# Layer 2's weights decoded in place, part of their lower halves on VectorE, and the first loads on ScalarE's queue, in a top-k attention and two-layer gated network kernel

## The chip, the cores and the metric

The program runs on one core of a Trainium2 chip. The metric is the device time of one execution in microseconds (us); the time before is 1244.49 us, the median of three runs (1243.4 to 1245.45). TensorE (PE in the profile) multiplies matrices into PSUM, VectorE (DVE), ScalarE (ACT) and GpSimd (POOL) work element by element on 128 partitions, SyncE (SP) issues the transfers.

## The reference, cut to what matters

```python
# q, k, v: (4, 8, 576, 64); all inputs arrive as float64
scores = q @ k.T / 8
mask   = scores >= (32nd largest of each row)
attn   = softmax(where(mask, scores, -1e9))
x      = (attn @ v) as 2304 tokens x 512
# layer 1, weights 512x1536, 512x1536, 1536x512
xn = x / sqrt(mean(x*x) + 1e-6) * rms_g
x  = (silu(xn @ w_gate) * (xn @ w_val)) @ w_out
# layer 2, weights of the same sizes
out = (sigmoid(x @ w_gate2) * (x @ w_val2)) @ w_out2
```

## The kernel before, in words

Every line of the profile reads L355, since one helper records all operations (`record`) and one place issues them (`issue`). The tiles' names tell the operations apart.

**A planner sets the order.** The program is first recorded as a list of operations with a priority each. `order` then plays a list schedule: five engines, a cost per operation (`cost`), rings of buffers, and for each engine the ready operation that can start soonest and, among those, the one of the lowest priority value. The engines get the operations in that order, so each engine's queue is fixed before the run. One planner rule touched by the change is the margin for TensorE: an operation of TensorE whose input ends after 250000 ns of planned time is held back by 1000 ns more (2500 ns where the input is a transfer), `SLACK`.

**Attention.** The 2304 tokens are 18 units of 128. A unit has 8 heads; one head of one unit is here called an *attend* (144 in all). An attend is: four score matmuls into `sp`; the largest eight (`MAX8` into `m`); the exponential on ScalarE (`e`); three rounds of `MATCH_REPLACE8` into the scratch tile `w` and `MAX8` of `w` on VectorE, which give the 32nd largest score; a masked product (`e<-sp,m,e`); a split in an upper half on ScalarE and a lower half on GpSimd (`ph`); a transposing transfer (`pt`) and 28 matmuls (`pv`). The scratch `w` has two buffers, and VectorE mostly runs two attends in turn.

**Layers.** Products run in float16 with operands split in an upper and a lower half, three matmuls for each product. Layer 1 (`gate1`, `out1`: tiles `pg<-xt`, `pw<-xt`, `py<-ht`) starts for a unit when its normalised rows `xt` are transposed. Layer 2 (`gate2`, `out2`: `pg<-yt`, `pw<-yt`, `po`) reads its weights from DRAM into tiles `wl` again for each batch of two units.

**Weights.** Each layer has nine pieces: three 512-wide parts (`j`) of gate, val and out (`g`, `v`, `o`), and a piece has four chunks of 128x512. A chunk arrives as 512 KB of float64 in a tile `raw` (128x512 pairs of 32-bit words), and `load_f32` turns the pairs into float32: for layer 2 (way 1) two ScalarE passes, one VectorE operation and one GpSimd addition. `prep_piece` then finds a power-of-two scale from a matmul of the piece with itself (`wps`, `wm`, `wmt`, `wx`), and makes the halves. Layer 1's halves stay in SBUF; its lower halves come from TensorE (`wlo`). For layer 2 (`prep2`, pieces `w2g`, `w2v`, `w2o`) the decoded float32 is written into a tile `wh`, which later takes the halves in its place: ScalarE scales into `wf` and rounds `wf` into the upper half, GpSimd subtracts the upper half from `wf`, and two stores per piece (512 KB each) bring it to DRAM. `raw`, `wh` and `wl` share one ring (`wbig`, tag `w4`) of seven buffers of 4 KB a partition. `gate2` keeps its gated rows in a ring of six smaller tiles (`htp`, tag `ht2`). All transfers are issued by SyncE, in its planned order; a transfer whose buffer is still in use holds up what is behind it there.

Of the kernel before, what the change touches and what calls it, by code (L numbers as in the profile page):

```python
# [9 lines left out]
F32 = mybir.dt.float32  # L10
F16 = mybir.dt.float16
BF16 = mybir.dt.bfloat16
I32 = mybir.dt.int32
# [28 lines left out]
HELD2 = False  # L42
REACH = 100.0
# [3 lines left out]
SLACK = (1000.0, 2500.0, 250000.0)  # L47
# [12 lines left out]
AHEAD = 8  # L60

# [39 lines left out]
class _Tile:  # L101
    def __init__(self, pool, args, key, lane):
        self.pool, self.args, self.key, self.lane = pool, args, key, lane
        self.real = None
        self.uses = []
        self.left = 0
        self.end = 0.0


class _Pool:  # L110
# [3 lines left out]
    def tile(self, shape, dtype, name, tag=None, bufs=None, lane=None):  # L114

        key = tag or name
        s = self.sched
        t = _Tile(self, (shape, dtype, f"{name}_{len(s.tiles)}", key, bufs), (id(self), key), lane)
        s.tiles.append(t)
        s.rings.setdefault(t.key, {"bufs": bufs or self.default, "lanes": {}})["lanes"].setdefault(lane, []).append(t)  # L120
        shadow = s.shadow.dram_tensor(f"t{len(s.tiles)}", list(shape), dtype).ap()
        return _View(t, shadow, [], [])


class _Op:
    __slots__ = "eng calls cost lat prio deps users waits tiles start end idx new later base".split()
# [10 lines left out]
class Scheduler:  # L137
# [67 lines left out]
    def cost(self, eng, method, args, kw, writes, reads):  # L205
# [16 lines left out]
        if eng == "scalar":  # L222
            return n * 0.8333 + (51 if psum else 93) + 93 * (ptrs + ("accum_out" in kw)), 200
        if eng == "gpsimd":
            if method == "tensor_tensor":
                return (516 if n == 1 else n * (1.88 if mybir.dt.size(out.dtype) == 2 else 2.1) + 149), 100
            return n * 0.833 + (224 if n == 1 else 161 + 300 * min(ptrs, 1)), 100

# [6 lines left out]
    def order(self):  # L235
        for op in self.ops:
            op.users, op.waits, op.start, op.end, op.new, op.later = [], len(op.deps), 0.0, None, [], []
# [35 lines left out]
        def choose(reach):  # L273
            best = None
            for eng in self.ENGINES:
                pick = None
                for op in ready[eng]:
# [10 lines left out]
                    key = (max(0.0, at - now[eng] - PATIENCE), op.prio, op.idx)  # L288
# [7 lines left out]
        while len(out) < len(self.ops):  # L296
# [16 lines left out]
            if op.eng == "sync":  # L313
# [4 lines left out]
                sems = sems[1:] + [done]  # L318
                if move:
                    op.end = begin + 56  # L320
# [38 lines left out]
def topk_attention_moe_kernel(  # L359
# [48 lines left out]
    wbig = pool("wbig", 7)  # L408
# [26 lines left out]
    def load_f32(dst, src, way):  # L435


        if src.dtype == F32:
            nc.sync.dma_start(dst, src)
            return  # L440
# [5 lines left out]
        E.claim(dst)  # L446
        if way == 1:
# [6 lines left out]
            return  # L454
# [4 lines left out]
        if way == 2:  # L459

            nc.scalar.activation(lo, lo.bitcast(U32), AF.Copy, scale=2.0 ** -29)
            nc.gpsimd.tensor_tensor(out=d, in0=d, in1=lo, op=ALU.add)
            return
# [4 lines left out]
    def prep_piece(w, kind, j, g, s, i, place, held, ways):  # L468
# [5 lines left out]
        for c in range(CPJ):  # L474
            r = (c if kind == "in" else j * CPJ + c) * P
            src = w[r : r + P, j * 512 : (j + 1) * 512] if kind == "in" else w[r : r + P, :]
            fs.append((held or place)(c).bitcast(F32))
            load_f32(fs[-1], src, ways[c])

        ps = ps_m.tile([P, P], F32, name="wps", tag="mm", lane="wps")  # L480
        with E.group():
            for c in range(CPJ):
                hb = fs[c].bitcast(BF16).rearrange("p (f a) -> p f a", a=2)[:, :, 1]
# [29 lines left out]
        for c in range(CPJ):  # L513
# [29 lines left out]
    def prep1(n, j):  # L543
# [9 lines left out]
        prep_piece(w, kind, j, g, s[:, j : j + 1], i[:, j : j + 1], lambda c: t[:, c], held, WAYS[0][len(pieces)])  # L553
        pieces.append([t[:, c] for c in range(CPJ)])

    def prep2(n, j):
# [3 lines left out]
        ts = [wbig.tile([P, 2, 1024], F16, name="wh", tag="w4") for _ in range(CPJ // 2)]  # L560
        held = None
        if HELD2:
            fs = [htp.tile([P, 2, CPJ, P], F16, name="fs", tag="ht2", bufs=6, lane="fs") for _ in range(CPJ)]
            held = lambda c: fs[c].rearrange("p a m r -> p (a m r)")
        prep_piece(w, kind, j, None, s[:, j : j + 1], i[:, j : j + 1], lambda c: ts[c // 2][:, c % 2], held, WAYS[1][len(pieces)])
        for a, t in enumerate(ts):
            nc.sync.dma_start(d[a], t.rearrange("p c f -> p (c f)"))
# [121 lines left out]
    def attend(parts, sc, nsc, pv, n):  # L689
# [12 lines left out]
        w = at.tile([P, S], F32, name="w", bufs=2)  # L702
# [297 lines left out]
    xs, dests, in1, in2, ht1, ht2, w2, hsq, ys, yts, state = {}, {}, {}, {}, {}, {}, {}, {}, {}, {}, {}  # L1000
# [106 lines left out]
```

## Time and profile before

| | |
|---|---|
| median of the runs | 1244.49 us |
| the profiled execution | 1248.31 us, of which the span of the profile is 1246.5 us |
| TensorE busy | 1128.9 us (91%) |
| VectorE busy | 999.0 us (80%) |
| ScalarE busy | 859.3 us (69%) |
| GpSimd busy | 844.8 us (68%) |
| first matmul that reads layer 2's weights | at 282.8 us |

The profile is one execution. Busy time is the sum of an engine's instructions; PEclk is the clock that TensorE was granted, as a share of its full 2.4 GHz. The span begins with the first instruction that is recorded; the execution's own time is 1.8 us more.

```profile
PE   4776484779899999999999999999999999999998
POOL 5997899986666667685877576566838666772530
PEclk9898576789999999999999999999999999999999
```

Each digit is one fortieth of the span (31 us) and gives the busy share in tenths. TensorE is not full in the first ten slices, while GpSimd is (and VectorE and ScalarE are too: the table of stretches further down); from the eleventh slice on TensorE is full to the end.

### The profile page before, as it was taken

The page shows a single profiled execution, that of the slowest core. Times are in us where ns is not written, and L with a number is a line of the kernel's source. Part 1 is how long each engine was busy: PE and PEld are TensorE (multiplying, and loading weights), DVE is VectorE, ACT ScalarE, POOL GpSimd, SP SyncE. Part 2 cuts the span into 40 slices and gives each one's busy share as a digit, 9 for nine tenths or more (in the row PEclk, how much of TensorE's full clock was granted, in tenths as well). Part 3 has the DMA queues.
Part 4 walks back from the last instruction along what each step waited for, and adds up shares of the span by engine and source line. Part 5 has one row for each costly group of instructions (what it writes and reads, how often), then busy time and mean ns, then how long its engine had stood idle before and what let it go on. Part 6 is the DMA issues. An engine that isn't in the chain of part 4 may idle for free.

```text
span 1246.5 us, 41715 instructions
## 1 busy us (share of the span) xinstructions
PE 1128.9 (91%) x17020; PEld 966.5 (78%) x17020; DVE 999.0 (80%) x2571; ACT 859.3 (69%) x1536; POOL 844.8 (68%) x966
## 2 busy tenths in 40 slices
PE   4776484779899999999999999999999999999998
PEld 2333273679699789978897999699879979997976
DVE  6999989798876998799989899798579899980001
ACT  6999788876676666676966576577748666763522
POOL 5997899986666667685877576566838666772530
PEclk9898576789999999999999999999999999999999
DMA  8995886889877775679877586868676865754337
GB/s 258 284 321 160 253 235 209 207 204 240 199 159 195 180 147 126 131 161 210 183 146 181 134 192 142 194 132 163 149 169 125 196 158 111 196 122 137 137 123 259
DMA packets 323776, 225.28 MB, mean 181 GB/s; under 512 B 278400, under 2 KB 286592, under 8 KB 323584
## 3 DMA queue, kind: packets, MB, share of 16 engines
q1 hardware_dynamic: 323584, 222.62, 73.1%
q8 instruction: 133, 2.18, 0.7%
q14 instruction: 59, 0.48, 0.1%
HBM read 147.06 MB, written 14.16 MB: 129 GB/s over the span
## 4 chain that ended last, share of the span: by engine, by line
PE 55%; DVE 14%; ACT 13%; issue 6%; POOL 6%; DMA 5%; SPq 2%; ACTq 0%; DVEq 0%; POOLq 0%
PE pg L355 14%; PE pw L355 14%; PE po L355 10%; PE py L355 8%; DVE m L355 5%; DVE w L355 5%; PE sp L355 3%; PE pv L355 3%; POOL ph L355 2%; SPq L355 2%; ACT raw L355 1%; ACT e L355 1%; ACT sg L355 1%; POOL sg L355 1%; DVE e L355 1%
## 5 line engine op out<-in xcount | busy, mean ns | idle before, releaser
L355 DVE MAX8 m<-w 128x8 f32<-128x576 f32 x432 | 315.0, 749 | 1.7
L355 PEld LDWEIGHTS <-wl 128*128 128x128 f16 x5184 | 292.5, 98 | 6.1 <-issue 4.7
L355 POOL TENSOR_TENSOR ph<-e,ph 128x512 f16<-128x512 f32 (+1 forms) x288 | 204.6, 735 | 77.5 <-ACT ph L355 75.9
L355 DVE MATCH_REPLACE8 w<-m,w 128x576 f32<-128x576 f32 x288 | 213.0, 742 | 0.0
L355 ACT ACTIVATE e<-sp,nb,sc 128x576 f32<-128x576 f32 x144 | 116.5, 829 | 75.5 <-POOL nb L355 41.7
L355 POOL TENSOR_TENSOR sg<-sg,sv 128x512 f32<-128x512 f32 x105 | 133.9, 1277 | 44.5 <-ACT sv L355 41.9
L355 PE MATMUL pg<-xt,w1g 128*128 128x128 f16 x2592 | 156.9, 221 | 1.2 <-DMA xt<-sn 0.4
L355 PE MATMUL pg<-yt,wl 128*128 128x128 f16 x2592 | 153.7, 219 | 3.6 <-ACT g L355 3.2
L355 PEld LDWEIGHTS <-w1v 128*128 128x128 f16 (+1 forms) x2640 | 150.1, 98 | 8.0 <-POOL w1v L355 4.3
L355 PEld LDWEIGHTS <-w1g 128*128 128x128 f16 (+1 forms) x2624 | 152.6, 99 | 3.6 <-issue 2.3
L355 PEld LDWEIGHTS <-w1o 128*128 128x128 f16 (+1 forms) x2640 | 152.6, 99 | 3.3 <-issue 1.8
L355 PE MATMUL pw<-yt,wl 128*128 128x128 f16 x2592 | 153.5, 219 | 1.1 <-ACT g L355 0.8
L355 PE MATMUL pw<-xt,w1v 128*128 128x128 f16 x2592 | 153.5, 219 | 0.3 <-ACT sv L355 0.3
L355 POOL TENSOR_TENSOR ht<-sg,ht 128x512 f16<-128x512 f32 x105 | 121.9, 1162 | 44.6 <-ACT ht L355 43.1
L355 PE MATMUL py<-ht,w1o 128*128 128x128 f16 x2592 | 150.0, 221 | 1.6 <-ACT acc L355 0.7
L355 PE MATMUL po<-wl,ht 128*128 128x512 f16 x648 | 146.5, 382 | 1.7 <-ACT g L355 1.7
L355 DVE MAX8 m<-sp 128x8 f32<-128x576 f32 x144 | 107.0, 757 | 40.6 <-PE sp L355 39.5
L355 ACT ACTIVATE ph<-e 128x576 f16<-128x576 f32 x144 | 96.5, 678 | 57.6 <-DVE e L355 52.8
L355 PE MATMUL sp<-kt,qt 128*128 128x512 f16 (+3 forms) x640 | 95.6, 300 | 33.6 <-DVE e L355 26.7
L355 DVE SCALAR_TENSOR_TENSOR e<-sp,m,e 128x576 f32<-128x576 f32 x144 | 115.3, 809 | 4.3 <-POOL wh L355 1.8
L355 PEld LDWEIGHTS <-ht 128*128 128x128 f16 x648 | 62.1, 98 | 72.5 <-issue 4.1
L355 ACT ACTIVATE ht<-sg 128x512 f16<-128x512 f32 x105 | 65.8, 627 | 70.1 <-POOL sg L355 69.7
(167 smaller groups left out, 1841.4 us busy)
## 6 DMA issues: line engine op xcount, KB each, us to landing
wl<-w2g SPq DMA_DIRECT2D x60, 512.0 KB, 5.0
wl<-w2v SPq DMA_DIRECT2D x60, 512.0 KB, 4.7
wl<-w2o SPq DMA_DIRECT2D x60, 512.0 KB, 5.3
raw<-in_moe_w_gate_dram SPq DMA_DIRECT2D x24, 512.0 KB, 5.1
raw<-in_moe_w_val_dram SPq DMA_DIRECT2D x24, 512.0 KB, 5.0
raw<-in_moe_w_out_dram SPq DMA_DIRECT2D x24, 512.0 KB, 5.4
qr<-in_q_dram SPq DMA_DIRECT2D x32, 128.0 KB, 3.7
kr<-in_k_dram SPq DMA_DIRECT2D x16, 256.0 KB, 4.1
```

The lines of the kernel that those rows point to most:

```text
L355: getattr(eng, method)(*map(real, a), **{n: real(x) for n, x in k.items()})
```

## The change

Layer 2's chunks are no longer decoded into `wh`. `load_f32` is called without a target and writes the float32 over the upper words of its own `raw` tile, every second word, where it stays until the halves are made. The halves go, chunk by chunk, into tiles of the `ht2` ring (named `wh` too), and are stored by four transfers of 256 KB for each piece. A list `LOW2` says for each of the nine pieces who makes the lower half: "p" as before (two ScalarE passes, GpSimd), "v" with one ScalarE pass straight into the upper half and one VectorE operation for the lower half. The ring `w4` has nine buffers in place of seven, the scratch `w` one in place of two. The first seven loads of `raw` are issued by ScalarE's queue. In the planner the margin for TensorE now holds from the start, and no longer delays an operation: it only counts when TensorE chooses among those that are ready.

```diff
+LOW1 = "ttttttttt"
+LOW2 = "vpvpvpvpv"
-SLACK = (1000.0, 2500.0, 250000.0)
+SLACK = (1000.0, 2500.0)
+FIRST = 7
...
-                    key = (max(0.0, at - now[eng] - PATIENCE), op.prio, op.idx)
+                    key = (max(0.0, max(at, op.safe if eng == "tensor" else 0.0) - now[eng] - PATIENCE), op.prio, op.idx)
...
-                late = SLACK[op.eng == "sync"] if u.eng == "tensor" and op.end > SLACK[2] else 0.0
-                u.start = max(u.start, op.end + OWN if u.eng == op.eng != "sync" else done + late)
+                late = SLACK[op.eng == "sync"] if u.eng == "tensor" else 0.0
+                u.start = max(u.start, op.end + OWN if u.eng == op.eng != "sync" and not op.calls[0][0].startswith("dma") else done)
+                u.safe = max(u.safe, done + late)
...
-    wbig = pool("wbig", 7)
+    wbig = pool("wbig", 9)
...
         raw = wbig.tile([P, 512, 2], I32, name="raw", tag="w4")
-        nc.sync.dma_start(raw.rearrange("p f a -> p (f a)"), src.bitcast(I32))
-        lo, hi, d = raw[:, :, 0], raw[:, :, 1], dst.bitcast(I32)
+        loads = (nc.scalar, nc.sync)[state["raws"] >= FIRST]
+        state["raws"] += 1
+        loads.dma_start(raw.rearrange("p f a -> p (f a)"), src.bitcast(I32))
+        lo, hi = raw[:, :, 0], raw[:, :, 1]
+        d = hi if dst is None else dst.bitcast(I32)
...
             if not held:
-                t = m1.tile([P, 512], F32, name="wf", tag="tmp", bufs=3, lane="wf")
-                nc.scalar.activation(t, fs[c], AF.Copy, scale=a)
-                nc.scalar.activation(hi, t, AF.Copy)
-                nc.gpsimd.tensor_tensor(out=lo, in0=t, in1=hi, op=ALU.subtract)
+                if how == "p":
+                    t = m1.tile([P, 512], F32, name="wf", tag="tmp", bufs=3, lane="wf")
+                    nc.scalar.activation(t, fs[c], AF.Copy, scale=a)
+                    nc.scalar.activation(hi, t, AF.Copy)
+                    nc.gpsimd.tensor_tensor(out=lo, in0=t, in1=hi, op=ALU.subtract)
+                    continue
+                nc.scalar.activation(hi, fs[c], AF.Copy, scale=a)
+                nc.vector.scalar_tensor_tensor(out=lo, in0=fs[c], scalar=a, in1=hi, op0=ALU.mult, op1=ALU.subtract)
+                continue
...
-        ts = [wbig.tile([P, 2, 1024], F16, name="wh", tag="w4") for _ in range(CPJ // 2)]
...
+                ts[c] = htp.tile([P, 2, CPJ, P], F16, name="wh", tag="ht2", bufs=6, lane="fs").rearrange("p a m r -> p (a m r)")
...
-        for a, t in enumerate(ts):
-            nc.sync.dma_start(d[a], t.rearrange("p c f -> p (c f)"))
+        for c in range(CPJ):
+            nc.sync.dma_start(d[c // 2, :, 1024 * (c % 2) : 1024 * (c % 2) + 1024], ts[c])
...
-        w = at.tile([P, S], F32, name="w", bufs=2)
+        w = at.tile([P, S], F32, name="w", bufs=1)
```

The matmul that finds the scale reads the upper 16 bits of each float32 (`high`); in the `raw` tile these lie 8 bytes apart, before they lay 4 bytes apart.

## Rows read from the trace of the kernel before

**Rows 1.** Busy time of each engine by stretch, then granted clock, DMA share, GB/s.

```profile
0.00:110.00 110.00, 74.75 (x381) 38.07 (x381) 96.79 (x263) 95.05 (x173) 89.76 (x106) 0.95 0.87 267
110.00:265.00 155.00, 94.02 (x1189) 78.08 (x1188) 141.68 (x373) 132.99 (x241) 139.59 (x147) 0.70 0.78 209
265.00:300.00 35.00, 30.59 (x498) 28.59 (x496) 29.74 (x91) 24.43 (x43) 24.13 (x30) 0.90 1.02 250
300.00:1100.00 800.00, 787.35 (x12909) 701.46 (x12907) 705.58 (x1785) 549.69 (x986) 540.29 (x637) 1.00 0.75 164
1100.00:1246.50 146.50, 142.24 (x2057) 120.25 (x2054) 25.19 (x65) 57.15 (x96) 51.06 (x48) 1.00 0.49 160
```

**Rows 2.** Groups of instructions from 0 to 300 us: count, busy us, mean ns, idle before.

```profile
L355 PE MATMUL pg<-xt,w1g 128*128 128x128 f16 x336 | 23.3, 238 | 0.7 <-DMA xt<-sn 0.4 <-DVE ws L355 0.3
L355 DVE MAX8 m<-sp 128x8 f32<-128x576 f32 x30 | 22.6, 756 | 1.2 <-PE sp L355 1.2
L355 PE MATMUL pg<-yt,wl 128*128 128x128 f16 x96 | 5.7, 219 | 0.0
```

**Rows 3.** Chain of waits in order of time: start, length, what.

```profile
969.05 8.06 PE py L355 x144
```

**Rows 4.** Timeline of all engines, first 22 us: start, length, what, idle before.

```profile
5.41 0.63 ACT L355 ACTIVATE gr<-gr 128x512 f32<-128x512 f32 x1 [3.41 <-DMA gr<-in_moe_rms_g_dram]
6.02 2.04 SPq L355 DMA_DIRECT2D raw<-in_moe_w_gate_dram  x4
```

**Rows 5.** Timeline of SyncE's queue: start, length, what it issued.

```profile
24.17 0.45 SPq L355 DMA_DIRECT2D raw<-in_moe_w_val_dram  x1
...
207.98 3.81 SPq L355 DMA_DIRECT2D w2o<-wh  x2
...
223.06 0.81 SPq L355 DMA_DIRECT2D raw<-in_moe_w_val_dram  x1
...
286.70 1.27 SPq L355 DMA_TRANSPOSE xt<-sn  x1
```

**Rows 6.** SyncE's own waits, 100 to 300 us: total us, times, longest.

```profile
SPq L355 <- POOL wh L355: 71.9, 32, 4.7
```

**Rows 7.** Groups of instructions over the span, shapes kept apart.

```profile
L355 POOL TENSOR_TENSOR wh<-wh,raw 128x512 int32<-128x512 int32 x36 | 46.5, 1296 | 8.8 <-ACT raw L355 4.2 <-ACT w1o L355 2.2 <-DVE w2vi L355 1.2
L355 POOL TENSOR_TENSOR wh<-wf,wh 128x512 f16<-128x512 f32 x36 | 41.0, 1163 | 3.9 <-ACT wh L355 3.7
L355 ACT ACTIVATE wf<-wh,ws 128x512 f32<-128x512 f32 x36 | 24.7, 714 | 0.0
L355 ACT ACTIVATE wh<-wf 128x512 f16<-128x512 f32 x36 | 21.3, 620 | 0.0
L355 PE MATMUL wps<-wh 128*128 128x128 bf16 x144 | 14.9, 270 | 17.3 <-POOL wh L355 10.2 <-DVE wh L355 7.1
L355 DVE SCALAR_TENSOR_TENSOR ht<-sg,c,ht 128x512 f16<-128x512 f32 x3 | 2.3, 751 | 2.4 <-ACT ht L355 2.4
```

**Rows 8.** Timelines of VectorE and GpSimd around 258 us.

```profile
258.47 1.06 DVE L355 TENSOR_TENSOR c<-w2vi,w2oi 128x3 f32<-128x3 f32 x1
258.24 1.27 POOL L355 TENSOR_TENSOR sg<-sg,sv 128x512 f32<-128x512 f32 x1
```

**Rows 9.** Timeline of VectorE: two attends in turn, then one attend alone.

```profile
450.26 1.41 DVE L355 MAX8 m<-w 128x8 f32<-128x576 f32 x2
451.59 0.07 DVE L355 MATCH_VALUE_LOAD w<-m,w 128x8 f32 x1
...
452.30 0.08 DVE L355 MATCH_VALUE_LOAD w<-m,w 128x8 f32 x1
...
487.42 0.09 DVE L355 MATCH_VALUE_LOAD w<-m,sp 128x8 f32 x1
...
488.35 0.76 DVE L355 MAX8 m<-w 128x8 f32<-128x576 f32 x1
489.15 0.09 DVE L355 MATCH_VALUE_LOAD w<-m,w 128x8 f32 x1
```

More of the change, by code (lines that the diff above doesn't have):

```diff
@@ L121, in tile @@
         shadow = s.shadow.dram_tensor(f"t{len(s.tiles)}", list(shape), dtype).ap()
+        t.shadow = shadow
         return _View(t, shadow, [], [])
 class _Op:
-    __slots__ = "eng calls cost lat prio deps users waits tiles start end idx new later base".split()
+    __slots__ = "eng calls cost lat prio deps users waits tiles start end idx new later base safe".split()
 class _Engine:
@@ L222, in cost @@
         if eng == "scalar":
+            if method == "dma_start":
+                return self.move(method, out, n)
             return n * 0.8333 + (51 if psum else 93) + 93 * (ptrs + ("accum_out" in kw)), 200
@@ L236, in order @@
         for op in self.ops:
-            op.users, op.waits, op.start, op.end, op.new, op.later = [], len(op.deps), 0.0, None, [], []
+            op.users, op.waits, op.start, op.end, op.new, op.later, op.safe = [], len(op.deps), 0.0, None, [], [], 0.0
         for op in self.ops:
@@ L466, in load_f32, with high, prep_piece @@
         )
-    def prep_piece(w, kind, j, g, s, i, place, held, ways):
+        return d.bitcast(F32)
+    def high(f):
+        if len(f.chain) and f.tile.args[2].startswith("raw"):
+            whole = _View(f.tile, f.tile.shadow, [], [])
+            return whole.rearrange("p f a -> p (f a)").bitcast(BF16).rearrange("p (f a) -> p f a", a=4)[:, :, 3]
+        return f.bitcast(BF16).rearrange("p (f a) -> p f a", a=2)[:, :, 1]
+    def prep_piece(w, kind, j, g, s, i, place, held, ways, how):
         fs = []
@@ L476, in prep_piece @@
             src = w[r : r + P, j * 512 : (j + 1) * 512] if kind == "in" else w[r : r + P, :]
-            fs.append((held or place)(c).bitcast(F32))
-            load_f32(fs[-1], src, ways[c])
+            fs.append(load_f32(None if held is None else held(c).bitcast(F32), src, ways[c]))
         ps = ps_m.tile([P, P], F32, name="wps", tag="mm", lane="wps")
@@ L517, in prep_piece @@
             if not held:
-                t = m1.tile([P, 512], F32, name="wf", tag="tmp", bufs=3, lane="wf")
-                nc.scalar.activation(t, fs[c], AF.Copy, scale=a)
-                nc.scalar.activation(hi, t, AF.Copy)
-                nc.gpsimd.tensor_tensor(out=lo, in0=t, in1=hi, op=ALU.subtract)
+                if how == "p":
[7 more added lines that the diff above has]
+                continue
+            if how == "v":
+                nc.scalar.activation(hi, fs[c], AF.Copy, scale=a)
+                nc.vector.scalar_tensor_tensor(out=lo, in0=fs[c], scalar=a, in1=hi, op0=ALU.mult, op1=ALU.subtract)
                 continue
@@ L552, in prep1 @@
         pieces, s, i = lay1[n]
-        prep_piece(w, kind, j, g, s[:, j : j + 1], i[:, j : j + 1], lambda c: t[:, c], held, WAYS[0][len(pieces)])
+        prep_piece(w, kind, j, g, s[:, j : j + 1], i[:, j : j + 1], lambda c: t[:, c], held, WAYS[0][3 * j + "gvo".index(n)], LOW1[3 * j + "gvo".index(n)])
         pieces.append([t[:, c] for c in range(CPJ)])
@@ L559, in prep2, with place @@
         d = dram.tile([CPJ // 2, P, 2048], F16, name=f"w2{n}{j}")
-        ts = [wbig.tile([P, 2, 1024], F16, name="wh", tag="w4") for _ in range(CPJ // 2)]
[L561 to L565, printed above, removed]
-        for a, t in enumerate(ts):
-            nc.sync.dma_start(d[a], t.rearrange("p c f -> p (c f)"))
+        ts = {}
+        def place(c):
+            if c not in ts:
+                ts[c] = htp.tile([P, 2, CPJ, P], F16, name="wh", tag="ht2", bufs=6, lane="fs").rearrange("p a m r -> p (a m r)")
+            return ts[c]
+        prep_piece(w, kind, j, None, s[:, j : j + 1], i[:, j : j + 1], place, None, WAYS[1][3 * j + "gvo".index(n)], LOW2[3 * j + "gvo".index(n)])
+        for c in range(CPJ):
+            nc.sync.dma_start(d[c // 2, :, 1024 * (c % 2) : 1024 * (c % 2) + 1024], ts[c])
         pieces.append(d)
```

23 lines of the change are left out of this document (15 added, 8 removed).

## The prediction

> **What bounds the kernel now.** I read the busy time by stretch first [rows 1]. From 300 us on TensorE is full: 787 of 800 us to 1100, then 142 of 146.5, at full clock. The end is therefore set by how much of TensorE's work is left at 300 us. Up to there it is not full: 74.8 us of 110, 94.0 of 155 at a granted clock of 0.70, 30.6 of 35 at 0.90. Busy time by clock gives 71 + 66 + 28 = 165 us of full-clock work in 300, so 135 us are lost before 300 us and 17 after. In that early part the other three engines are the full ones: from 110 to 265 us VectorE is busy 141.7 of 155, GpSimd 139.6, ScalarE 133.0. These are the weights' preparation and the first attends.
>
> What TensorE lacks early is ready work, and later it has too much of it. By 300 us 30 attends (3.75 units) have begun, but layer 1 has seen 336/144 = 2.33 units and layer 2 only 96/144 = 0.67 [rows 2]. A unit takes 3 x 144 matmul times in a layer, 3 x 8.06 = 24.2 us [rows 3]. Three whole units thus leave 0.67 + 2.33 = 3 layers, 72 us of layer work, waiting at 300 us. So the next microseconds are to be had from layer 2's weights coming sooner, and a few from the start; an attend that comes somewhat later costs nothing while that heap lasts.
>
> **The change part by part.** *The first loads.* SyncE issues the first `raw` load at 6.02 us, behind the loads of q, k and v; four issues take 2.04 us, 0.51 each [rows 4]. ScalarE is idle for 3.41 us before 5.41 us [rows 4], and seven issues are 3.6 us, so 0.2 us stick out, ahead of the first square. The loads leave some 4 us sooner, and the eighth, which stood at 24.17 us behind a transposing transfer and two loads [rows 5], finds one of the nine buffers free at about 6 us. Against it: q, k and v now share the DMA engines with 3.7 MB more. Bounds 0 and -4 us on all that follows; I take -3, since VectorE's decoding starts with these loads.
>
> *Layer 2's preparation.* It is a loop over buffers. SyncE spends 71.9 us between 100 and 300 us behind GpSimd's operations on `wh` [rows 6]; after the stores of a piece at 207.98 us the last load of the piece two further on leaves at 223.06 [rows 5]. With nine buffers, none held by halves, a piece's four loads follow each other as the halves of the piece two before are made. Then GpSimd's and ScalarE's work is what paces. Five of nine pieces, 20 chunks, lose a GpSimd subtraction of 1.163 us each (23.3 us) and a ScalarE pass of 0.620 (12.4 us); the remaining pass with its scale costs what `wf` costs, 0.714 [rows 7]. VectorE gains 20 operations; the same form on the last unit's rows takes 0.751 us [rows 7], 15.0 us in all.
>
> *But this VectorE operation reads two SBUF tiles.* At 258.47 us a product of two SBUF tiles, three columns wide, takes 1.06 us and ends at 259.53; a GpSimd addition that began at 258.24 ends at 259.51 [rows 8]. VectorE stood still until GpSimd had finished. The three rows of 0.751 us come from the tail, where GpSimd has nothing to do. With GpSimd busy nine tenths of this stretch and its operations at some 1.2 us, each of the 20 waits about half of one, 0.54 us: 10.8 us more on VectorE, 26 in all, between 15 (no wait) and 15 + 20 x 1.2 = 39. The other way round a GpSimd operation that comes up during the 0.75 us waits a part of it, some 0.35 us, 7 us in all. Of GpSimd's 23.3 us some 16 remain.
>
> The Trainium skill says the same in "SBUF — State Buffer", section "Who interferes with whom": a VectorE instruction with two SBUF inputs contends with a GpSimd instruction that reads SBUF, and the later one blocks fully. By that rule the trace agrees, with the 1.06 us above; without the rule the relief would be 23.3 us.
>
> So layer 2's weights are ready 16 us sooner (bounds 0 and 23.3). TensorE's rate before they come is 66/155 = 0.42 up to 265 us and 28/35 = 0.79 after; between the two, 0.6, so 0.4 of each microsecond is won: -6.4 us (bounds 0 and -23.3, the latter if attention comes sooner by as much).
>
> *VectorE's 26 us* exceed its 13 idle us of this stretch, and attends give way. Unit 2's rows are transposed at 286.70 us [rows 5] and may come 10 to 15 us later. The waiting 72 us cover that after 300 us; before it some layer 1 work moves back. I take +2 (0 to +6).
>
> *In place, with steps of 8 bytes.* GpSimd's addition already reads one input with that step, in 1.296 us [rows 7]; with three such operands I take the same (bounds: 36 x 0.1 us either way). The 144 matmuls for the scale take 0.27 us each [rows 7]; even at twice that, 39 us more would fall in a stretch where TensorE is idle 61 us [rows 1], partly on the piece's own chain, 4.3 us a piece: 0, at worst +3.
>
> *Stores.* Eighteen more issues on SyncE lie in 155 us; they wait in order for halves, as the two did, and transposing transfers behind them wait with them. The last half of a piece decides as before: 0 (-1 to +2).
>
> *One scratch tile.* Two attends in turn need 1.33 us for two `MAX8`, 0.665 each, and 0.71 us from one value load to the next. An attend alone needs 0.80 from `MAX8` to the value load and 0.93 from the value load to `MAX8` [rows 9]. That is 0.13 and 0.22 more, three times each per attend: 1.05 us at most. The next attend's first `MAX8`, the masked product of the one before, and small operations can stand in most gaps. I take 0.4 us, 46 us over the 114 attends after 300 us, where VectorE is idle 94 of 800 us [rows 1]: 0, at worst the rival below.
>
> *TensorE's margin* only reorders; from 300 us on TensorE has 17 idle us in all [rows 1]. I take 0 (-3 to +3).
>
> Sum: -3 - 6.4 + 2 = -7.4 us on the profiled execution, 1248.3 to 1240.9 (its span 1246.5 to 1239.1). It lies 3.8 us above the median; from the median, 1244.5 - 7.4 = 1237.
>
> **The rivals.** *The whole early part shrinks* (0.17). GpSimd also makes each attend's bias and lower half, and if it is what holds attention too, units come sooner with the weights: -3 and the full 16 to 23 us, some -20, 1224 us. For it speaks that all three engines are at about 90%, so none has much to give; against it that VectorE gets work where it is the fullest.
>
> *VectorE takes over what GpSimd gives up* (0.19). If the 20 waits come to 1.2 us each, and decoding stands behind them in VectorE's queue, the pieces come no sooner: only the start remains, less the 2 us, about -1: 1243.5 us, no change that can be told. This is the mechanism of the 1.06 us row; the skill's page named above would have it so whenever GpSimd is always busy.
>
> *The single scratch tile makes VectorE the bound* (0.21). Attention ends soon after 1100 us, since VectorE has 25 us of work left there [rows 1]; the 142 us of TensorE's work after it [rows 1] hold layer 2 of two units, layer 1 and layer 2 of the last one, 4 x 24.2 = 97, so there are 45 us to spare. If half the gaps stay open, 0.55 us, and VectorE's idle time does not take them because it consists of waits for TensorE's scores, attention ends 63 us later, 18 beyond what can be spared; less 8 of gain that is +10, 1254 us. It decides from 45 us of delay on, 0.4 us an attend. For it speaks that VectorE is 88% busy from 300 to 1100; against it that its order is planned with the gap between dependent operations counted.
>
> That a part does nothing at all (ScalarE's loads leaving no sooner) takes 3 us off the forecast and stays inside its range.
>
> **How the numbers follow.** The forecast has 0.43, with a range of its own of 1230 to 1242. From both sides the cases reach 1224 and 1254; leaving out a part of each, the range is 1222 to 1252. A change of 0.2%, 2.5 us, is about what a measurement here can tell. Faster than 1242: 0.41 of the forecast, the 0.17, and 0.02 of the no-change case, 0.60. Within: 0.02 and 0.16, 0.18. Slower: 0.21 and 0.01, 0.22.
>
> **What would show it.** Right: `raw` loads at 2 us on ScalarE's queue; 16 GpSimd subtractions for `wh` in place of 36; the new VectorE group of 20 with a mean near 1.3 us; the last store of `w2o` before 250 us (265 now), layer 2's first matmul near 265 (283 now), and TensorE's lost time before 300 us down by about 8. Wrong: a mean of 0.75 us there (no waiting), a last store at 260 us or later, or TensorE idle for more than 25 us after 300 us with scores waiting for VectorE.

## The result, and the profile after

The changed kernel takes 1258.0 us (median of 4 runs, 1256.6 to 1259.5) against 1244.4 us (1243.4 to 1245.5) in the same comparison: a ratio of 1.0116, 95% interval 1.0099 to 1.0133. It is 1.2% slower, where 1237 us, 0.6% faster, was forecast. The profiled execution took 1257.94 us, with a span of 1256.2 us; before, 1248.31 and 1246.5 us.

The busy time by stretch answers to [rows 1], with the stretch from 300 us cut at 400 us (columns as there: TensorE, its weight loads, VectorE, ScalarE, GpSimd, granted clock, DMA share, GB/s).

```profile
0.00:110.00 110.00, 67.21 (x334) 35.24 (x335) 90.48 (x244) 90.17 (x165) 86.86 (x103) 0.94 0.86 273
110.00:265.00 155.00, 91.26 (x1106) 76.92 (x1105) 147.08 (x383) 126.71 (x220) 109.23 (x125) 0.70 0.81 228
265.00:300.00 35.00, 35.00 (x638) 33.62 (x636) 33.74 (x83) 22.63 (x41) 23.79 (x29) 1.00 1.11 248
300.00:400.00 100.00, 88.52 (x1415) 79.49 (x1414) 88.16 (x229) 69.28 (x128) 64.29 (x76) 0.91 0.67 153
400.00:1100.00 700.00, 693.55 (x11303) 617.18 (x11301) 638.88 (x1553) 473.93 (x853) 472.53 (x557) 1.00 0.73 160
1100.00:1256.20 156.20, 152.21 (x2236) 129.65 (x2234) 45.38 (x103) 66.07 (x110) 58.36 (x60) 1.00 0.50 153
```

The same cut of the kernel before:

```profile
300.00:400.00 100.00, 94.67 (x1607) 85.26 (x1605) 77.27 (x208) 73.09 (x135) 68.10 (x76) 0.98 0.86 199
400.00:1100.00 700.00, 692.68 (x11306) 616.19 (x11303) 628.31 (x1578) 476.60 (x852) 472.19 (x561) 1.00 0.73 159
```

From 400 to 1100 us the two are alike: 693.6 and 692.7 of 700 us. The loss is ahead of that. Up to 110 us all engines do less (TensorE 67.2 us instead of 74.8, VectorE 90.5 instead of 96.8), from 110 to 265 us VectorE has 5.4 us more work and GpSimd 30.4 us less (23.3 us of subtractions were to go), and from 300 to 400 us TensorE is busy 88.5 us at a clock of 0.91 instead of 94.7 at 0.98. I call *lost time* what a 10 us window is longer than TensorE's busy time in it by the granted clock. Summed, it is 130.2 us to 300 us, 6.7 to 400 and 11.7 after in the kernel before, and 132.5, 18.5 and 10.4 in the changed one: 12.8 us more, of which 11.8 fall between 300 and 400 us. The measure is good to a few us: the two spans differ by 9.7 us, the medians by 13.6. A count says the same: by 400 us TensorE has run 3487 of its 17020 matmuls, 182 fewer than before, and at 62 ns each (700 us over 11303) these are 11.3 us.

The start, on ScalarE's queue and TensorE (timeline: start, length, what, idle before), answers to [rows 4]:

```profile
0.72 9.51 ACTq L368 DMA_DIRECT2D raw<-in_moe_w_gate_dram  x4
...
10.73 1.31 ACTq L368 DMA_DIRECT2D raw<-in_moe_w_val_dram  x3
...
12.07 1.28 ACT L368 ACT_TABLE_LOAD   x1 [12.07 <-issue]
...
18.94 1.33 PE L368 MATMUL wps<-w1v 128*128 128x128 bf16 x11 [18.94 <-DVE w1v L368]
```

The loads begin at 0.72 us, but four issues take 9.51 us. ScalarE's table load, at 0.72 us before, comes at 12.07, and TensorE's first matmul, at 7.87 before, at 18.94. In the listing of the program's instructions, engine by engine, the reason stands beside the fourth load:

```
## ACT: 1376 rows
3 L368 DMA raw_124<-in_moe_w_gate_dram 128x1024
4 L368 DMA raw_128<-in_moe_w_gate_dram 128x1024 [waits DMAHW3_49]
5 L368 DMA raw_132<-in_moe_w_val_dram 128x1024 [waits DMAHW5_49]
...
## SP: 655 rows
5 L368 DMA kr_130<-in_k_dram 64x64
6 L368 DMA kr_130<-in_k_dram 64x64 [waits DMAHW0_49]
```

A semaphore is a counter that is raised when a piece of work ends and that others wait for. In this program eight of them tell the ends of transfers, in turn, whichever of the two queues issues them. From the ninth transfer on (of the first eight, three were ScalarE's and five SyncE's), an issue waits for the transfer that had its semaphore last. For the fourth load that is the first load of q, issued at 1.77 us; loads of q take up to 8.1 us from issue to landing, and the fourth load leaves at 9.90 us. The planner keeps count of the semaphores for SyncE alone.

The groups of instructions over the span, shapes apart (count, then busy us, mean ns, idle before), answer to [rows 7]:

```profile
L368 POOL TENSOR_TENSOR raw<-raw 128x512 int32<-128x512 int32 x36 | 37.7, 1053 | 19.1 <-DVE raw L368 11.2 <-DVE p2t L368 1.9 <-issue 1.7
...
L368 PE MATMUL wps<-raw 128*128 128x128 bf16 x144 | 18.8, 297 | 9.5 <-DVE raw L368 5.1 <-DVE ws L368 3.0 <-POOL raw L368 1.4
L368 POOL TENSOR_TENSOR wh<-wf,wh 128x512 f16<-128x512 f32 x16 | 18.3, 1163 | 0.6 <-ACT wh L368 0.4
...
L368 DVE SCALAR_TENSOR_TENSOR wh<-raw,ws,wh 128x512 f16<-128x512 f32 x20 | 17.3, 922 | 0.0
...
L368 ACT ACTIVATE wh<-raw,ws 128x512 f16<-128x512 f32 x20 | 13.6, 751 | 4.8 <-DVE ws L368 4.8
...
L368 ACT ACTIVATE wf<-raw,ws 128x512 f32<-128x512 f32 x16 | 11.5, 743 | 0.0
```

The change does what it says: 16 subtractions on GpSimd, 20 on VectorE. Their mean there is 922 ns: 18.4 us by count, or 17.3 where overlaps count once. Their median is 743 ns, the longest took 1644, beside a GpSimd operation that had begun before it:

```profile
213.35 1.64 DVE L368 SCALAR_TENSOR_TENSOR wh<-raw,ws,wh 128x512 f16<-128x512 f32 x1
...
212.96 1.48 POOL L368 TENSOR_TENSOR ht<-sg,ht 128x512 f16<-128x512 f32 x1 [0.75 <-ACT ht L368]
```

SyncE's queue around layer 2's weights and the rows of units 2 and 3 answers to [rows 5]; then unit 3 of the kernel before:

```profile
242.36 2.36 SPq L368 DMA_DIRECT2D w2o<-wh  x4
...
306.47 1.59 SPq L368 DMA_TRANSPOSE xt<-sn  x1
...
370.20 1.34 SPq L368 DMA_TRANSPOSE xt<-sn  x1
```

```profile
342.99 1.23 SPq L355 DMA_TRANSPOSE xt<-sn  x1
```

The last store of `w2o` leaves at 244.4 us (the fourth of these), 21 us sooner than before, and layer 2's first matmul is at 258.6 us instead of 282.9. But unit 2's rows are transposed 19.8 us later and unit 3's 27.2 us later. The groups up to 300 us answer to [rows 2]:

```profile
L368 PE MATMUL pg<-xt,w1g 128*128 128x128 f16 x288 | 20.8, 242 | 1.7 <-ACT sf L368 1.3 <-DVE wx L368 0.2 <-DVE raw L368 0.2
...
L368 PE MATMUL pg<-yt,wl 128*128 128x128 f16 x144 | 8.5, 219 | 0.0
```

```profile
L368 DVE MAX8 m<-sp 128x8 f32<-128x576 f32 x28 | 21.1, 753 | 5.0 <-PE sp L368 5.0
```

Two units through layer 1 and one through layer 2, 28 attends begun instead of 30. Up to 340 us the layers stand as before (432 and 192 against 432 and 178 of the same matmuls), but 34 attends have begun instead of 36. Then TensorE's windows:

```profile
320.00:330.00 10.00, 10.00 (x184) 9.76 (x182) 9.69 (x21) 7.77 (x16) 7.50 (x9) 1.00 0.62 114
330.00:340.00 10.00, 5.54 (x98) 4.72 (x94) 9.74 (x23) 7.62 (x16) 9.29 (x11) 0.92 0.53 102
340.00:350.00 10.00, 9.88 (x132) 9.34 (x133) 9.69 (x24) 3.81 (x7) 4.64 (x7) 0.74 0.44 91
350.00:360.00 10.00, 7.23 (x116) 6.20 (x114) 6.95 (x29) 4.67 (x10) 2.23 (x4) 0.77 0.52 88
360.00:370.00 10.00, 8.44 (x124) 8.11 (x124) 9.04 (x29) 9.34 (x18) 7.96 (x9) 0.72 0.40 93
370.00:380.00 10.00, 7.50 (x138) 7.06 (x135) 9.59 (x30) 8.53 (x16) 6.70 (x7) 1.00 0.99 279
```

In 330 to 340 us, 4.5 us are empty while VectorE is busy 9.74 of 10. Then the clock is granted at 0.72 to 0.77, a mix of its two levels of 1.2 and 2.4 GHz, for 30 us; by the definition above that is 6.6 of the 18.5 us lost here. What TensorE's first idle times wait for is attention's own work, not weights (timeline of TensorE, idle time before in brackets; then SyncE's queue):

```profile
337.52 0.38 PE L368 MATMUL kvt<-kvn,ones 128*128 128x1 f32 x2 [2.37 <-ACT ks L368]
340.12 1.18 PE L368 MATMUL sp<-kt,qt 128*64 128x512 f16 x8 [2.22 <-DVE kvi L368]
...
360.71 0.37 PE L368 MATMUL pg<-yt,wl 128*128 128x128 f16 x2 [1.15 <-ACT yt L368]
...
395.97 2.85 PE L368 MATMUL pg<-yt,wl 128*128 128x128 f16 x48
398.66 2.84 PE L368 MATMUL pw<-yt,wl 128*128 128x128 f16 x48
```

```profile
312.88 0.84 SPq L368 DMA_DIRECT2D wl<-w2v  x2
```

Nor was other work lacking. By the program, 360.71 us is unit 2's first piece of layer 2, and 395.97 and 398.66 us are unit 1's second, 5.7 us long. Unit 1's rows were in use from 306.42 us on, and the last of these weights were issued at 312.88 us. But the kernel runs layer 2 of two units piece by piece in turn, and TensorE takes its queue in the order that was fixed before the run.

### The profile page after: what moved, and what is told of

Same layout as the page of the kernel before. It is cut to its first block, busy times and chain, and to the rows that moved or that the text cites. A ratio compares the mean times of both kernels' runs of the same rounds, so it can differ in the third digit from the quotient of the medians.

```text
span 1256.2 us, 41653 instructions
## 1 busy us (share of the span) xinstructions
PE 1127.7 (90%) x17020; PEld 972.1 (77%) x17020; DVE 1043.7 (83%) x2591; ACT 848.8 (68%) x1516; POOL 815.1 (65%) x946
## 4 chain that ended last, share of the span: by engine, by line
PE 57%; DVE 14%; POOL 7%; issue 5%; ACT 4%; DMA 1%; POOLq 0%; DVEq 0%; ACTq 0%
PE pg L368 17%; PE pw L368 16%; PE py L368 9%; PE po L368 9%; DVE m L368 5%; DVE w L368 4%; PE sp L368 3%; PE pv L368 3%; POOL sg L368 2%; POOL ph L368 2%; DVE e L368 2%; POOL ht L368 1%; DVE wh L368 1%; DVE raw L368 1%; ACT e L368 1%
## 5 line engine op out<-in xcount | busy, mean ns | idle before, releaser
L368 DVE MAX8 m<-w 128x8 f32<-128x576 f32 x432 | 326.9, 757 | 11.0
L368 PEld LDWEIGHTS <-qt 128*128 128x128 f16 (+1 forms) x640 | 51.3, 103 | 96.5 <-DVE e L368 34.5
```

The lines of the kernel that those rows point to most:

```text
L368: getattr(eng, method)(*map(real, a), **{n: real(x) for n, x in k.items()})
```

## The experiments

Each is compared with the kernel before, run beside it on the same chip. The kernel before took 1242.8 to 1244.7 us in these sessions, so variants of different sessions are compared by their ratios. The first ones undo one part of the change; START, HELD, LOAD and RUSH in the expectations are these theories. START: ScalarE, held by its own issues, starts everything late. HELD: decoding in place costs by itself, as a raw tile stays taken from its load until its halves are made. LOAD: the 20 operations on VectorE displace attends. RUSH: layer 2's preparation, with more tiles free, runs ahead of the attends. HALVES is an earlier name of LOAD; the other names are explained where they stand.

**First loads back on SyncE** (from the changed kernel).

```diff
-FIRST = 7
+FIRST = 0
```

> The changed kernel with all loads of raw on SyncE's queue again. Theory START (ScalarE's queue stands until 12.07 us behind its seven loads, three of which leave by 2.1 us and the fourth only at 9.90, so the whole early part begins some 10 us late and the units arrive late): about 1246 us, 10 to 12 less than the changed kernel's 1258, and the first unit's rows are transposed near 170 us (185.2 in the changed kernel, 164.0 before). Theory SCRATCH (one scratch tile slows each attend) and theory HALVES (the 20 VectorE halves displace attends): no less than 1254 us, first unit's rows still later than 178 us.

1254.3 us, 1.0096 [1.0076, 1.0116]. 3.7 us between the medians (2.5 by the ratios), and the intervals overlap: little of the 13.6 us. The first unit's rows come at 177.7 us, not at 170.

**Two scratch tiles** (from the changed kernel; a tile less in the ring pays for it).

```diff
-    wbig = pool("wbig", 9)
+    wbig = pool("wbig", 8)
-        w = at.tile([P, S], F32, name="w", bufs=1)
+        w = at.tile([P, S], F32, name="w", bufs=2)
```

> The changed kernel with two scratch tiles w again; for lack of room the ring of raw and wl has 8 buffers in place of 9. SCRATCH: 1250 us or less, VectorE's mean start-to-start of an attend shorter, the last attend done 15 us or more sooner than at 1149 us. START and HALVES: 1255 to 1261 us.

1255.9 us, 1.0112 [1.0088, 1.0135]: no change that can be told. The single tile, set against a ninth tile in the ring, is not what makes the changed kernel slow.

**All halves on GpSimd** (from the changed kernel).

```diff
-LOW2 = "vpvpvpvpv"
+LOW2 = "ppppppppp"
```

> The changed kernel with all nine pieces' lower halves on GpSimd, as before the change. HALVES: 1252 us or less, and units 1 to 3 arrive 5 us or more sooner than at 245.7, 306.5 and 370.2 us. START and SCRATCH: 1256 to 1264 us, with layer 2's first matmul 5 to 15 us later than at 258.6 us.

1263.5 us, 1.0162 [1.0142, 1.0181]. Slower: LOAD falls here, the VectorE halves help within the change.

**The seven loads alone** (on the kernel before, with the planner's part for them).

```diff
-        nc.sync.dma_start(raw.rearrange("p f a -> p (f a)"), src.bitcast(I32))
+        loads = (nc.scalar, nc.sync)[state["raws"] >= FIRST]
+        state["raws"] += 1
+        loads.dma_start(raw.rearrange("p f a -> p (f a)"), src.bitcast(I32))
```

> The kernel before with nothing changed but the first seven loads of raw on ScalarE's queue. START: 1253 us or more, ScalarE's first activation after 10 us (5.4 before). SCRATCH and HALVES: 1242 to 1247 us, no change.

1262.4 us, 1.0160 [1.0145, 1.0175]: 20 us slower, more than the whole change, though undoing it there gave 3.7. What the parts cost does not add.

**The margin alone, and the margin undone** (on the kernel before; from the changed kernel).

```diff
-                    key = (max(0.0, at - now[eng] - PATIENCE), op.prio, op.idx)
+                    key = (max(0.0, max(at, op.safe if eng == "tensor" else 0.0) - now[eng] - PATIENCE), op.prio, op.idx)
...
```

> The kernel before with nothing changed but the planner's margin for TensorE (from the start, as a preference). Theory MARGIN (the new order of work is what costs, since undoing the loads, the scratch or the halves gave back little): 1249 us or more, unit 3's rows later than at 350 us (342.99 before). Theory ARRIVAL (TensorE runs dry between 330 and 380 us because unit 3's rows are late, and what makes them late is work and waits put ahead of them on ScalarE and VectorE): 1240 to 1248 us, unit 3 at 340 to 350 us.

> The changed kernel with the planner's old margin (none up to 250 us, then a real delay). MARGIN: 1250 us or less. ARRIVAL: 1255 to 1261 us, unit 3's rows after 360 us as in the changed kernel (370.2).

Alone 1250.6 us, 1.0058 [1.0036, 1.0079], with runs from 1246.7 (the profiled one) to 1256.0. Undone, 1263.8 us, 1.0152 [1.0137, 1.0167]. On one kernel it costs, on the other it helps.

**One scratch tile alone** (on the kernel before).

```diff
-        w = at.tile([P, S], F32, name="w", bufs=2)
+        w = at.tile([P, S], F32, name="w", bufs=1)
```

> The kernel before with nothing changed but one scratch tile w in place of two. SCRATCH: 1250 us or more, the last attend done after 1140 us (1105 to 1128 before). ARRIVAL without SCRATCH: 1242 to 1248 us.

1247.9 us, 1.0028 [1.0014, 1.0042]: 3.5 us.

**In place alone, and in place with the VectorE halves** (on the kernel before: the float32 stays in `raw`, halves in the gated rows' ring, 8 raw tiles, two scratch tiles, SyncE's loads, the old margin).

```diff
+LOW2 = "ppppppppp"
...
-    wbig = pool("wbig", 7)
+    wbig = pool("wbig", 8)
...
+        d = hi if dst is None else dst.bitcast(I32)
...
+                ts[c] = htp.tile([P, 2, CPJ, P], F16, name="wh", tag="ht2", bufs=6, lane="fs").rearrange("p a m r -> p (a m r)")
...
```

The second has `LOW2 = "vpvpvpvpv"`.

> The kernel before with only the decoding in place (8 buffers; all lower halves on GpSimd, loads on SyncE, two scratch tiles, old margin). LOAD (the 20 operations on VectorE make the attends late): 1241 to 1248 us, 25 or more attends begun by 265 us. HELD (decoding in place itself costs: raw tiles stay taken from the load to the halves, and the halves take the ring of the gated rows): 1252 us or more.

> The kernel before with only the decoding in place and the five pieces' VectorE halves: loads on SyncE, two scratch tiles, old margin; the ring of raw and wl has 8 buffers, for lack of room. The forecast's own mechanism (layer 2's weights sooner is time won): 1234 to 1240 us. ARRIVAL: layer 2's first matmul before 260 us (282.9 before) and yet 1243 us or more, with the loss moved to 330 to 390 us.

1256.9 us, 1.0101 [1.0067, 1.0135], and 1259.2 us, 1.0111 [1.0096, 1.0126]. Decoding in place alone costs as much as the whole change. Its trace: VectorE's own waits (total us, times, longest) from 60 to 265 us, then the busy time by stretch.

```profile
DVE raw L368 <- ACT raw L368: 9.3, 8, 4.8
DVE wm L368 <- PE wps L368: 4.4, 5, 1.3
DVE p2t L368 <- ACT qn L368: 3.4, 1, 3.4
```

```profile
110.00:265.00 155.00, 91.91 (x1042) 74.91 (x1043) 129.36 (x351) 135.18 (x237) 128.53 (x143) 0.70 0.83 232
```

VectorE is busy 129.4 of 155 us (141.7 before), and the attends begun by 265 us are 22 instead of 26. It is not fuller, it waits more: 27.2 us in all from 60 to 265 us, against 12.9 before; for ScalarE's pass over `raw` 9.3 us (the like wait before was 6.1), for the scale's matmuls 4.4. The changed kernel does not show this: there VectorE waits 8.7 us in the same time.

**The VectorE halves alone** (on the kernel before; from `wf`, pieces 1, 3, 5, 7 and 9).

```diff
-                nc.gpsimd.tensor_tensor(out=lo, in0=t, in1=hi, op=ALU.subtract)
+                eng = nc.vector if how == "v" else nc.gpsimd
+                eng.tensor_tensor(out=lo, in0=t, in1=hi, op=ALU.subtract)
```

> The kernel before with only the lower halves of pieces 1, 3, 5, 7 and 9 subtracted on VectorE in place of GpSimd (from wf, both inputs in SBUF; nothing in place, ring of 7). LOAD: 1249 us or more, 24 attends or fewer begun by 265 us. HELD: 1240 to 1247 us.

1242.3 us, 0.9989 [0.9977, 1.0002]. Not told from no change, and the only variant not slower. Groups, then the stretch:

```profile
L355 DVE TENSOR_TENSOR wh<-wf,wh 128x512 f16<-128x512 f32 x20 | 16.8, 871 | 0.5 <-ACT wh L355 0.5
```

```profile
110.00:265.00 155.00, 97.98 (x1265) 84.50 (x1263) 149.30 (x393) 138.75 (x251) 128.12 (x133) 0.74 0.86 233
```

20 operations of 871 ns on VectorE, which is busy 7.6 us more than before in this stretch. Its idle time took a part of the 17 us.

**No halves at all** (in place; the 20 VectorE operations replaced by a fill with zeros, so these lower halves are left out of the result).

```diff
-                nc.vector.scalar_tensor_tensor(out=lo, in0=fs[c], scalar=a, in1=hi, op0=ALU.mult, op1=ALU.subtract)
+                nc.vector.memset(lo, 0.0)
```

> The in-place kernel with five pieces on VectorE (1259 us), its 20 operations for the lower halves replaced by a fill with zeros, so these lower halves are left out. LOAD: 1250 us or less, 25 attends or more begun by 265 us. HELD: 1254 us or more.

1253.0 us, 1.0068 [1.0045, 1.0091], with a fill of 272 ns in place of some 900. With two thirds of LOAD taken away (5.4 us of VectorE's time are left of 17.4), in place still costs 8.5 us: HELD stands, as the cost of decoding in place, whatever its inside.

**Three loads on ScalarE** (as the seven, where nothing waits for a semaphore).

```diff
-FIRST = 7
+FIRST = 3
```

> The kernel before with the first three loads of raw, not seven, on ScalarE's queue: these three were issued without a wait in the changed kernel. START (what costs is that ScalarE's table load and first work stand behind loads that wait for other transfers' semaphores): ScalarE's table load by 2.5 us (12.07 with seven), and 1240 to 1246 us, against 1262 with seven. If sharing the transfer engines is what costs: 1250 us or more.

1255.8 us, 1.0091 [1.0071, 1.0111]. ScalarE's start, then the stretches of this kernel and of the kernel before:

```profile
0.72 1.39 ACTq L363 DMA_DIRECT2D raw<-in_moe_w_gate_dram  x3
...
2.14 1.28 ACT L363 ACT_TABLE_LOAD   x1 [2.14 <-issue]
```

```profile
0.00:20.00 20.00, 3.34 (x21) 2.67 (x21) 11.27 (x29) 12.05 (x21) 10.09 (x14) 1.00 0.82 281
20.00:265.00 245.00, 153.26 (x1348) 102.32 (x1349) 213.42 (x576) 208.13 (x376) 209.48 (x229) 0.76 0.79 224
```

```profile
0.00:20.00 20.00, 3.40 (x20) 2.53 (x20) 10.54 (x28) 11.98 (x21) 11.58 (x16) 1.00 0.85 249
20.00:265.00 245.00, 165.37 (x1548) 113.62 (x1549) 227.93 (x608) 216.06 (x393) 217.77 (x238) 0.79 0.82 232
```

The table load comes at 2.14 us and the first 20 us are as full as before on TensorE, VectorE and ScalarE. From 20 to 265 us VectorE has 14.5 us less work and TensorE 12.1 less. With seven loads on the kernel before these 20 us lack more: VectorE is busy 7.6 us, ScalarE 6.4, GpSimd 6.0 (10.5, 12.0 and 11.6 without). So START, as a delay by blocking, explains those 3 to 6 us at the start, but not the 11 us that three loads cost. Nor does the delay last: with seven loads TensorE's lost time to 300 us is 127.8 us, less than the 130.2 of the kernel before, and the cost stands in the next 100 us, 26.9 against 6.7. I put it down to the order that the planner made from other starting times; no run shows that apart. That the transfers of the first loads disturb others was not tried by itself either.

**Layer 2's preparation later, and rings of other sizes.** With a step of 0.3 for 0.1 between the priorities of layer 2's nine pieces, so that the later ones give way to attends (from the changed kernel with its loads on SyncE; from in place with halves), a ring of 7 for 8 (in place with halves), and one of 8 for 7 (kernel before).

```diff
-PREP2 = (0.6, 0.1)
+PREP2 = (0.6, 0.3)
```

> The changed kernel with all loads on SyncE and layer 2's nine pieces planned further apart (priority step 0.3 in place of 0.1 of a unit, so the later pieces give way to attends). Theory RUSH (a larger ring lets layer 2's preparation, whose priority is above that of units 1 to 3, run ahead of attends; by 265 us 24 attends in place of 26): units 1 to 3 arrive 8 us or more sooner than at 247, 302, 363 us, layer 2's first matmul later than at 243 us, and 1240 to 1249 us in all. Theory LOAD (it is only the work added on VectorE): 1251 to 1257 us.

> As the in-place kernel with 8 buffers (1259 us) and layer 2's pieces planned further apart (step 0.3). RUSH: 1250 us or less, 25 or more attends begun by 265 us. LOAD: 1255 to 1262 us.

> In place and five pieces' halves on VectorE, on the kernel before (loads on SyncE, two scratch tiles, old margin), with the ring of raw and wl left at 7 buffers; with 8 it took 1259 us. RUSH: 1252 us or less, 25 or 26 attends begun by 265 us (23 with 8 buffers), layer 2's first matmul after 265 us. LOAD: 1255 to 1262 us.

> The kernel before with nothing changed but 8 buffers of raw, wh and wl in place of 7. RUSH: layer 2's first matmul 8 us or more sooner than at 282.9, fewer than 26 attends begun by 265 us, and 1247 us or more. LOAD: 1241 to 1246 us.

1253.2 us, 1.0072 [1.0044, 1.0099]; 1263.1 us, 1.0143 [1.0105, 1.0182]; 1266.4 us, 1.0172 [1.0139, 1.0206]; 1245.6 us, 1.0016 [0.9997, 1.0034]. In the first two layer 2 starts at 285 and 295 us and nothing that can be told is regained; a smaller ring costs more, and a larger one on the kernel before nothing that can be told. RUSH falls as an account of the time, though what it says of the order is seen: the larger ring brings layer 2 forward by 7.9 us with 24 attends begun by 265 us instead of 26, and in the first run units 1 to 3 do come 7 to 14 us sooner than without the wider step.

**Two last ones.** In place alone with the changed kernel's nine tiles and single scratch tile; and the VectorE halves alone with a step of 0.2, in search of a version that beats both.

```diff
-    wbig = pool("wbig", 8)
+    wbig = pool("wbig", 9)
-        w = at.tile([P, S], F32, name="w", bufs=2)
+        w = at.tile([P, S], F32, name="w", bufs=1)
...
-PREP2 = (0.6, 0.1)
+PREP2 = (0.6, 0.2)
```

> Decoding in place alone, which with 8 raw tiles and two scratch tiles took 1256.9 us, now with 9 raw tiles and one scratch tile, as the changed kernel has them (a single scratch tile alone cost 3.5 us on the kernel before). If what costs is that a raw tile stays taken from its load until its halves are made, the ninth tile gives back a part: SyncE's loads of layer 2's raw tiles run further ahead, unit 3's rows come by 350 us, 1246 to 1252 us. If the ring's size is not the limit (order or the 8-byte steps are): 1255 to 1263 us, unit 3 at 355 us or later.

> The kernel before with the halves of pieces 1, 3, 5, 7 and 9 subtracted on VectorE (which alone gave 1242.3 us), and layer 2's preparation due a little later (PREP2 0.2 in place of 0.1), so that attends come first where both are ready. Theory (the arrival of units 1 to 3 decides, weights that come sooner are not time won): units 1 to 3 transposed no later than 225, 289 and 342 us, 1235 to 1242 us. Rival (weights sooner are time won, so later weights cost): 1246 to 1255 us. That any new order of these instructions costs some microseconds by chance: 1244 to 1250 us with units 1 to 3 later.

1255.5 us, 1.0087 [1.0070, 1.0103], unit 3 at 356.75 us: the number of tiles is not the limit, and HELD in the form "the ring is too small" falls as the main cause. (The ninth tile was paid for with the scratch tile, 3.5 us alone, so it may give back some 5.) 1244.6 us, 1.0008 [0.9996, 1.0020], units 1 to 3 at 236.6, 298.7 and 346.5 us: they came later although the preparation that competes with them came later too, which is the third case of the expectation. The operations are those of the variant of 1242.3 us, only the order differs; the two ratios are at the edge of what can be told apart. No version here beats the kernel before.

All runs together (rows of units 2 and 3 transposed, layer 2's first matmul, TensorE's lost time to 400 us, all in us from the profiled executions):

| kernel | ratio | unit 2 | unit 3 | layer 2 | lost |
|---|---|---|---|---|---|
| before | 1 | 287 | 343 | 283 | 137 |
| before + halves on VectorE | 0.999 | 289 | 342 | 257 | 130 |
| same, step 0.2 | 1.001 | 299 | 346 | 277 | 129 |
| before, ring of 8 | 1.002 | 298 | 350 | 275 | 143 |
| before + one scratch tile | 1.003 | 291 | 350 | 265 | 136 |
| before + margin | 1.006 | 285 | 342 | 275 | 137 |
| in place, fill for halves | 1.007 | 297 | 364 | 261 | 147 |
| after, SyncE's loads, step 0.3 | 1.007 | 295 | 349 | 285 | 138 |
| in place, nine tiles | 1.009 | 298 | 357 | 257 | 146 |
| before + 3 loads | 1.009 | 309 | 359 | 276 | 154 |
| after, SyncE's loads | 1.010 | 302 | 363 | 243 | 142 |
| in place | 1.010 | 308 | 360 | 263 | 146 |
| in place + halves | 1.011 | 305 | 355 | 256 | 145 |
| after, two scratch tiles | 1.011 | 309 | 363 | 258 | 149 |
| after | 1.012 | 306 | 370 | 259 | 151 |
| in place + halves, step 0.3 | 1.014 | 303 | 357 | 295 | 150 |
| after, old margin | 1.015 | 304 | 361 | 243 | 149 |
| before + 7 loads | 1.016 | 304 | 358 | 265 | 155 |
| after, no VectorE halves | 1.016 | 312 | 380 | 255 | 158 |
| in place + halves, ring of 7 | 1.017 | 292 | 356 | 300 | 153 |

The order of the ratios is not that of layer 2's start: 257 us stands at 0.999 and 1.009, 243 us at 1.010 and 1.015. It goes with the units: up to 1.006 unit 3 comes by 350 us, and of the 14 others 13 have it at 355 us (rounded) or later. The fourteenth has it at 349 us and is 9 us slower than the kernel before all the same. What parts the two groups without exception is the count of matmuls that TensorE has run by 400 us: 3623 to 3788 in the six, 3305 to 3577 in the 14. So the difference between the groups is made by then; that it is made because unit 3 comes late is inferred from the table and from TensorE's windows, and no run delayed that unit by itself. Every kernel that decodes in place or loads on ScalarE is at 1.007 or above, every other within 1.006.

## Why the prediction was wrong

**The step that failed** is the sentence on VectorE's 26 us: unit 2's rows "may come 10 to 15 us later. The waiting 72 us cover that after 300 us". They came 19.8 us later, and the 72 us did not cover it, for two reasons. The figure counted three whole units at 300 us, from attends begun. Layer 1 can take a unit only once its rows are transposed, and in the changed kernel that is two units at 300 us: four layers less the two and one that were done leave one, 24 us, and the third unit's rows only come at 306.47 us. By the same count both kernels have done three layers by then, so it is the late unit that is missing, not work that the sooner layer 2 had used up. And the heap was taken as work for any idle moment. TensorE first stood at 335 us, when unit 2's rows were there and some 50 us of the layers of units 1 and 2 (an estimate, 24.2 us a layer) were undone; part waited for unit 2's own steps, and at least 5.7 us were ready and stood further back in TensorE's fixed queue until 395.97 us. So an attend that came later did cost time.

By 340 us as much layer work was done as before and two attends fewer. An attend is some 6.2 us of VectorE (705.6 us for the 114 after 300 us, [rows 1]), so two are 12.4 us; that this is near to the 12.8 us of TensorE's lost time proves nothing by itself. What made the units late is shown only by parts: decoding in place or the first loads on ScalarE, each alone, do it; how they do it is open.

*Layer 2's preparation* was sized well and valued wrong. 16 us sooner were forecast, 24 came by the first matmul, 21 by the last store. The halves alone (257 us) and in place alone (263 us) each bring as much, so the relief of GpSimd is not its only source. -6.4 us rested on TensorE's rate with and without the weights, as if rows were always there for them. The halves alone, with layer 2 starting as early, gain at most 0.2%.

*In place* was put at 0, at worst +3; alone it is +12.6 us. The prices per operation held within a tenth or were better: GpSimd's addition 1.05 us instead of 1.30, the scale's matmuls 297 ns instead of 270, the pass to `wf` 743 instead of 714. Alone, the cost shows as VectorE's waiting, which a sum over operations doesn't hold. Why it waits more there is open: a larger ring did not cure it, later preparation did not, taking two thirds of the halves' VectorE work away cured some 5 of 14 us. In the changed kernel VectorE does not wait more. Up to 265 us it is as busy as before (237.6 and 238.5 us), 17.3 us of it for the halves, and 23 attends have begun instead of 26. Yet with the halves back on GpSimd it was slower still. The 8-byte steps, the halves' new ring and the 18 more stores were not tried one by one. SyncE's waits behind `wh` did fall, against 71.9 us of [rows 6] (100 to 300 us):

```profile
SPq L368 <- DVE wh L368: 12.5, 11, 4.4
SPq L368 <- POOL wh L368: 11.7, 11, 2.0
```

*First loads*: -3 (0 to -4) had the wrong sign, even outside its bounds: alone they cost 20 us, in the change 2.5 to 3.7. The issues were counted at 0.51 us from [rows 4], and that one of them could wait for a transfer was not seen. That accounts for what the first 20 us of the run lack; the case of three loads shows a cost without it.

*VectorE's halves*: 922 ns instead of 1.3 us, 0.18 us of waiting over the median's 743, not 0.54. The rule of the Trainium skill's "SBUF — State Buffer", "Who interferes with whom", that the later of the two blocks, fits single ones, as the pair of lines at 213 us above; the median shows that most did not wait. In the nine other kernels with such halves the mean runs from 780 to 1144 ns, so 0.18 us is not a fixed price. The rival in which VectorE takes over what GpSimd gives, at 1.2 us of waiting each, falls with it.

*Single scratch tile*: the sum's 0 held closer than the rival's +18. Groups over the span, after and before:

```profile
L368 DVE MAX8 m<-w 128x8 f32<-128x576 f32 x432 | 326.9, 757 | 11.0
```

```profile
L355 DVE MAX8 m<-w 128x8 f32<-128x576 f32 x432 | 315.0, 749 | 1.7
```

VectorE's idle time before these `MAX8` grows by 9.3 us, and from 1100 us it has 45.4 us of work left instead of 25.2, but TensorE loses no more after 400 us (10.4 against 11.7). The rival's time, 1254 us, is near the result for a reason that isn't its own. Alone the part costs 3.5 us.

*Margin*: 0 (-3 to +3) held in neither direction, +7 alone, and 4 to 6 us slower without it in the changed kernel. *Stores*: no run tried them apart. *The whole early part shrinks*: the rows of units 0 to 3 came 9 to 27 us later, so it falls.

Of the marks set ahead, the first loads at 0.72 us, 16 subtractions and the last store before 250 us came true, without the time following; the mean near 1.3 us did not. The one that caught it was TensorE's lost time before 300 us: it should have fallen by 8 and rose by 2.3.

## What to carry to other kernels

Before valuing an input that comes sooner, count what it can be used on at that time, in the unit that the consumer takes (here whole units with rows transposed), and ask which engine would make the other input and whether the same edit slows that. Where a program orders the instructions, price each part alone on the chip and expect a new order to be worth some microseconds either way: the planner's margin, which changes the order alone, cost 0.6% on one kernel and saved 0.4% on another, and parts worth +20, +13, +7, +3.5 and -1.4 us alone made 14 together. A DMA issue on a computing engine holds that engine for as long as the issue waits.

## What the runs showed of the hardware

- In this program the queues of SyncE and ScalarE share eight completion semaphores in turn: seven issues on ScalarE, 3.6 us at the 0.51 us of [rows 4], took until 12.04 us.
- A VectorE operation on two SBUF inputs beside a GpSimd that is busy 70 to 83% of the stretch took 922 and 871 ns on average in two kernels; the medians are 743 and 684. In the other kernels with it the means are 780 to 1144 ns.
- A GpSimd addition of 128x512 int32 with all three operands at 8-byte steps in one tile took 1.05 us; with one input at that step and the other operands in a second tile at 4-byte steps, 1.30 us [rows 7]. Step and tile were not tried apart.
